# Some softmax reciprocals moved from VectorE to ScalarE, the instruction order given as a table, and the first loads reordered, in a two-layer linear-attention and gated-MLP kernel

## The chip, the core and the metric

The kernel runs on one core of a Trainium2 chip. The metric is the device time of one execution in microseconds (us). The engines are TensorE (PE, with its weight loads PEld), VectorE (DVE), ScalarE (ACT), GpSimd (POOL) and SyncE (SP), whose queue issues DMAs; ACT's queue issues some DMAs too.

## The reference

Inputs are bfloat16: `x` of 2048 rows by 512, and weights. Two blocks, A and B, alternate twice: A, B, A, B, each added to `x` after a layer normalisation without gain.

```python
# A: linear attention, H = 32 heads of Dh = 16
qkv = (x @ wqkv) ...                          # q, k, v: [b, h, s, d]
pq = einsum("bhsd,hdf->bhsf", q, w_phi);  pk = einsum("bhsd,hdf->bhsf", k, w_phi)
phi_q = concat([softmax(pq), softmax(-pq)]);  phi_k = concat([softmax(pk), softmax(-pk)])
kv = einsum("bhsf,bhsd->bhfd", phi_k, v);     z = einsum("bhsf->bhf", phi_k)
num = einsum("bhqf,bhfd->bhqd", phi_q, kv);   den = einsum("bhqf,bhf->bhq", phi_q, z)[..., None] + 1e-6
A = (num / den) @ wo
# B: gated MLP, F = 1376
gate = x @ W_gate;  up = x @ W_up
B = (gate * (gate > 0) * up) @ W_down
```

## The kernel before

`x` stays in SBUF as `X`, 16 tiles of 128 rows; four tiles are a chunk. For each layer:

- **Norm**: bn_stats and bn_aggr on DVE give mean and variance of a tile; POOL takes (variance + eps) to the power -1/2 into `rstd`; the tile is normalised on ACT, DVE or POOL and transposed, by a DMA of the SP queue or by PE. Some chunks of layer 1 take the two sums from accumulators instead (`sums`).
- **Folding**: the feature weights `w_phi` are multiplied into the key and query parts of `wqkv` (`Wk2`, `Wq2`), the key part by PE transposes, the query part by two DMA transposes of `wq`.
- **Keys and values** (`keys_values`, group k): PE projects a tile, ACT takes exp(p) and exp(-p) into `ek`, DVE (some of it after a halving add on POOL) sums each softmax into `sk`, DVE inverts the 128x64 sums into `rk`, and POOL and DVE share the scaling of `ek` by `rk`. PE adds up `kv` over all 16 tiles, values beside a column of ones (`vext`). `build_R` masks `kv` into `R` on DVE.
- **Queries** (`queries`, group q): the same with one scaling by the quotient of the two sums (`rq`), and a DMA transpose.
- **Attention** (groups a and p): PE multiplies by `R`; DVE inverts the denominators (`dd`) and scales; a transpose; PE multiplies by `wo`; DVE adds to `X`, with the row sum as accumulator; **Centre** takes the mean off.
- **The gated MLP** (`glu`, groups g and d): 10 column tiles of gate and up, by chunk, cut into parts (`PARTS`); ACT and DVE form the product; PE multiplies by `W_down`, DVE adds to `X`.

The program is first written down as a list of some 1,900 operations (`Plan.op`), each with engine, estimated time, what it reads and writes. `Plan.order` then walks through an estimated time and lets each engine take the ready operation with the highest rank, with a bias for each group and engine from the table `RANK`. The operations are emitted in that order; each engine runs its own in order. `STEP` holds, tile by tile, which engine does what: `kr` and `qr` the way of summing (`1` one DVE reduction over both halves, `2` two, `H` and `P` with one or two halving adds on POOL), `ks` how many of eight parts of the key scaling POOL takes, `part0` the cuts of the MLP chunks, `turn` which first tiles PE transposes, `wake` how many matmuls of zeros PE runs.

Of the kernel before, what the change touches and what calls it, by code (L numbers as in the profile page):

```python
# [8 lines left out]
P = 128  # L9
D = 512  # L10
H = 32
DH = 16
F = 1376
NDB = D // P
# [36 lines left out]
TAIL = {"PE": 0.165, "ACT": 0.12, "DVE": 0.115, "POOL": 0.045, "SP": 0.0}  # L51
SAME = {"PE": -0.165, "ACT": 0.035, "DVE": 0.035, "POOL": 0.08, "SP": 0.0}
HOPS = {("DVE", "POOL"): 0.09, ("ACT", "POOL"): 0.15}
NEXT = {"PE": 0.055, "SP": 0.03}
FREE = 0.06


def hop(a, b):
    return SAME[a] if a == b else HOPS.get((a, b), NEXT.get(b, 0.04))


class Plan:
# [10 lines left out]
    def op(self, eng, occ, fn, reads=(), writes=(), holds=(), lat=0.0, at=0.0, group=None, port=False, long=False):  # L73

        o = Op()
        o.eng, o.occ, o.cost, o.fn, o.lat, o.at, o.port, o.long = eng, occ, occ + TAIL[eng], fn, lat, at, port, long
        o.group, o.i_in = group or self.group
        base, slope = RANK.get(f"{o.group}.{eng}") or RANK[o.group]
        o.bias = base - slope * o.i_in
        o.preds, o.succs, o.i = set(), [], len(self.ops)  # L80
# [18 lines left out]
    def order(self):  # L99
        for o in self.ops:  # L100
            for p in o.preds:
                p.succs.append(o)
        for o in reversed(self.ops):
            o.rank = o.cost + o.lat + max([s.rank + hop(o.eng, s.eng) for s in o.succs], default=0.0)
        free = {k: [0.0] * n for k, (pool, n) in self.kinds.items()}
        engines = sorted({o.eng for o in self.ops})
        busy = {e: 0.0 for e in engines}
        ready = {e: [] for e in engines}
        for o in self.ops:
            o.wait, o.t0 = len(o.preds), o.at  # L110
            if not o.wait:
                ready[o.eng].append(o)
        seq, left, now, shut = [], len(self.ops), 0.0, 0.0
        while left:
            moved, later = False, []
            for e in engines:
                if busy[e] > now + 1e-9:
                    later.append(busy[e])
                    continue
                best = None  # L120
                for o in ready[e]:
                    if o.t0 > now + 1e-9:
                        later.append(o.t0)
                        continue
                    if o.port and shut > now + 1e-9:
                        later.append(shut)
                        continue
                    ok = True
                    need = {}
                    for b in o.bufs:  # L130
                        if b.slot is None:
                            need[b.kind] = need.get(b.kind, 0) + 1
                    for k, n in need.items():
                        got = [t for t in free[k] if t is not None]
                        if len(got) < n:
                            ok = False
                        else:
                            t = sorted(got)[n - 1]
                            if t > now + 1e-9:
                                later.append(t)  # L140
                                ok = False
                    if ok and (best is None or (o.rank + o.bias, -o.i) > (best.rank + best.bias, -best.i)):
                        best = o
                if best is None:
                    continue
                o = best
                ready[e].remove(o)
                moved, left = True, left - 1
                o.start, end = now, now + o.cost
                busy[e] = now + o.occ  # L150
                if o.long:
                    shut = end
                later.append(busy[e])
                for b in o.bufs:
                    if b.slot is None:
                        b.slot = min((i for i, t in enumerate(free[b.kind]) if t is not None),
                                     key=lambda i: free[b.kind][i])
                        free[b.kind][b.slot] = None
                        b.end = 0.0
                    b.left -= 1  # L160
                    b.end = max(b.end, end + o.lat + FREE)
                    if not b.left:
                        free[b.kind][b.slot] = b.end
                for s in o.succs:
                    s.wait -= 1
                    s.t0 = max(s.t0, end + o.lat + hop(e, s.eng))
                    if not s.wait:
                        ready[s.eng].append(s)
                seq.append(o)
            if not moved:  # L170
                later = [t for t in later if t > now + 1e-9]
                assert later, "the plan is stuck"
                now = min(later)
        self.seq = seq
        return seq
# [15 lines left out]
WF_IN, WK_IN, WV_IN, WQ_IN, LOADED = 3.4, 4.2, 6.7, 10.4, 11.0  # L191
X_IN = [3.3, 4.5] + [5.2] * 2 + [7.4] * 4 + [8.9] * 4 + [11.8] * 4
# [8 lines left out]
def setup(ctx, tc, A_x, A_wqkv, A_w_phi, A_wo, B_W_gate, B_W_up, B_W_down, out):  # L201
# [28 lines left out]
    nc.sync.dma_start(out=wkv[:, :, D:2 * D], in_=wv[:, :, 2 * D:3 * D])  # L230
    st.X, st.wkv, st.wq = X, wkv, wq

    st.zero = const.tile([P, D], BF16, name="zero")
    nc.vector.memset(st.zero[:], 0.0)
    wake = const.tile([P, 1], F32, name="wake")
    nc.scalar.activation(out=wake[:], in_=st.zero[:, 0:1], func=AF.Exp)
    nc.scalar.dma_start(out=X[:, 4:8, :], in_=xv[:, 4:8, :])
    nc.scalar.dma_start(out=X[:, 8:12, :], in_=xv[:, 8:12, :])
    nc.scalar.dma_start(out=wq[:], in_=wv[:, :, 0:D])
    nc.scalar.dma_start(out=X[:, 12:16, :], in_=xv[:, 12:16, :])  # L240
# [456 lines left out]
def keys_values(st, c, xnT, kv, L, last_er=()):  # L697

    nc, pl = st.nc, st.pl
    for ti in range(TPC):  # L700
# [21 lines left out]
        def invert(sk=sk, rk=rk):  # L722
            with nc.allow_low_precision(reason="the reference keeps a softmax and its sums in bfloat16"):
                nc.vector.reciprocal(out=rk[:], in_=sk[:])  # L724
# [284 lines left out]
```

## Time and profile before

| what | value |
|---|---|
| median of three runs | 381.89 us (381.57 to 382.64) |
| the profiled execution | 380.91 us, its span 379.2 us |
| busy: PE / DVE / ACT / POOL | 363.6 / 268.0 / 205.5 / 121.1 us |
| DMA, whole span | 32.61 MB, mean 86 GB/s |

The span is the time from the first to the last instruction in the trace; 1.7 us of the execution's own time lie outside it. Busy time is the union of an engine's instructions, an idle time is put down to what ended it.

### The profile page before, as it was taken

The numbers are of one execution on the slowest core, as the hardware profiler recorded it, in microseconds if no ns is written. First come the engines' busy times: TensorE is split into PE (matmuls) and PEld (weight loads), VectorE is DVE, ScalarE is ACT, GpSimd is POOL, SyncE is SP. The second block draws the span as 40 slices with busy tenths as digits, with TensorE's granted clock in tenths as the row PEclk, the third lists the DMA queues.
The fourth block names the chain that finished last, engine by engine and source line by source line (L and its number), as shares of the span: only waits on it lengthen the run. The fifth ranks groups of instructions, "written<-read, shape, count | busy, mean of one in ns | idle before, by whom it ended". The sixth has DMA issues, their size and how long they took to land.

```text
span 379.2 us, 6724 instructions
## 1 busy us (share of the span) xinstructions
PE 363.6 (96%) x2380; PEld 189.9 (50%) x2409; DVE 268.0 (71%) x608; ACT 205.5 (54%) x439; POOL 121.1 (32%) x203
## 2 busy tenths in 40 slices
PE   4898999999899999999999999999999999999996
PEld 2444545756445444444444456475654445454444
DVE  4999999999925442763497998999962675172433
ACT  4898979776762446737706925865234135514100
POOL 3798965131110220560155681724310002000000
PEclk9999999999999999999999999999999999999999
DMA  8889936788950230021013070478930075000011
GB/s 262 239 143 227 260 44 144 133 149 146 145 107 2 42 58 15 0 30 27 0 22 77 9 119 3 87 127 146 171 85 14 5 146 115 14 0 16 1 55 57
DMA packets 98882, 32.61 MB, mean 86 GB/s; under 512 B 90560, under 2 KB 98336, under 8 KB 98848
## 3 DMA queue, kind: packets, MB, share of 16 engines
q1 hardware_dynamic: 97216, 29.93, 39.7%
q10 hardware_dynamic: 1632, 2.24, 1.8%
q8 instruction: 19, 0.31, 0.4%
q14 instruction: 15, 0.12, 0.1%
HBM read 8.44 MB, written 2.10 MB: 28 GB/s over the span
## 4 chain that ended last, share of the span: by engine, by line
PE 64%; DVE 24%; DMA 6%; issue 2%; ACT 1%; POOL 1%; SPq 0%; POOLq 0%; ACTq 0%
PE ps L613 37%; PE ps L645 14%; PE ps L884 5%; DMA b<-b 4%; DVE sk L682 4%; DVE rk L724 3%; DVE bnst L388 3%; PE ps L794 3%; PE ps L593 3%; DVE sk L692 2%; DVE b L730 2%; PE q L833 2%; DMA X<-in_A_x_dram 2%; DVE sq L682 1%; DVE sk L688 1%
## 5 line engine op out<-in xcount | busy, mean ns | idle before, releaser
L613 PE MATMUL ps<-b,wu 128*128 128x512 bf16 (+2 forms) x400 | 79.2, 336 | 0.6 <-DMA b<-b 0.6
L613 PE MATMUL ps<-b,wg 128*128 128x512 bf16 (+2 forms) x400 | 78.6, 336 | 0.0
L645 PE MATMUL ps<-wd,b 128*128 128x512 bf16 (+3 forms) x368 | 78.1, 366 | 0.3
L623 ACT ACTIVATE b<-ps 128x512 bf16<-128x512 f32 (+2 forms) x100 | 50.5, 520 | 39.6 <-PE ps L613 39.1
L626 DVE SCALAR_TENSOR_TENSOR b<-ps,b 128x512 bf16<-128x512 f32 (+2 forms) x60 | 35.1, 598 | 39.9 <-PE ps L613 38.9
L645 PEld LDWEIGHTS <-b 128*128 128x128 bf16 (+1 forms) x374 | 35.3, 98 | 39.1
L613 PEld LDWEIGHTS <-wg 128*128 128x128 bf16 x400 | 36.1, 98 | 33.1
L613 PEld LDWEIGHTS <-wu 128*128 128x128 bf16 x400 | 36.2, 98 | 32.7 <-issue 0.9
L730 POOL TENSOR_TENSOR b<-b,rk 128x1024 bf16<-128x1024 bf16 (+6 forms) x28 | 37.5, 1351 | 9.6 <-DVE rk L724 7.9
L798 ACT ACTIVATE b<-ps 128x512 bf16<-128x512 f32 x64 | 33.0, 638 | 5.7 <-PE ps L794 5.1
L715 ACT ACTIVATE b<-ps 128x512 bf16<-128x512 f32 x64 | 33.7, 628 | 1.3 <-PE ps L710 1.3
L679 POOL TENSOR_TENSOR b<-b 128x256 f32<-128x256 bf16 x30 | 19.7, 670 | 43.9 <-ACT b L715 34.1
L570 DVE SCALAR_TENSOR_TENSOR X<-ps,r,X 128x512 bf16<-128x512 f32 (+2 forms) x26 | 18.2, 701 | 20.2 <-PE ps L645 20.1
L710 PE MATMUL ps<-Wk,b 128*128 128x512 bf16 x123 | 29.4, 379 | 2.0 <-DMA b<-b 1.2
L884 PE MATMUL ps<-wo,b 128*128 128x512 bf16 x118 | 29.7, 379 | 1.5 <-DMA b<-b 0.9
L630 DVE TENSOR_TENSOR b<-b,b 128x512 bf16<-128x512 bf16 (+2 forms) x40 | 13.5, 348 | 24.0 <-ACT b L623 22.3
L552 POOL TENSOR_SCALAR ve<-tot 128x4 f32<-128x4 f32 x8 | 1.9, 233 | 88.8 <-ACT sq L548 88.8
L663 PE MATMUL ps<-wkv,b 128*128 128x512 bf16 x122 | 29.9, 386 | 0.3
L794 PE MATMUL ps<-Wq,b 128*128 128x512 bf16 x126 | 29.5, 379 | 0.1
L548 ACT ACTIVATE sq<-b 128x512 bf16<-128x512 bf16 x32 | 20.1, 627 | 17.4 <-DVE b L527 17.0
L598 ACT CAST ur<-ps 128x192 bf16<-128x192 f32 (+1 forms) x18 | 5.4, 302 | 32.2 <-PE ps L593 32.1
L814 POOL TENSOR_TENSOR b<-b,rq 128x512 bf16<-128x512 bf16 x19 | 20.2, 1061 | 8.4 <-DVE rq L807 6.1
(94 smaller groups left out, 493.7 us busy)
## 6 DMA issues: line engine op xcount, KB each, us to landing
out_dram<-X SPq DMA_DIRECT2D x15, 128.0 KB, 1.8
X<-in_A_x_dram ACTq DMA_DIRECT2D x3, 512.0 KB, 7.2
b<-b SPq DMA_TRANSPOSE x94, 3.2
wg<-in_B_W_gate_dram SPq DMA_DIRECT2D x8, 160.0 KB, 3.2
wu<-in_B_W_up_dram SPq DMA_DIRECT2D x8, 160.0 KB, 4.0
wd<-in_B_W_down_dram SPq DMA_DIRECT2D x5, 256.0 KB, 4.7
wkv<-in_A_wqkv_dram SPq DMA_DIRECT2D x2, 512.0 KB, 7.1
wq<-in_A_wqkv_dram ACTq DMA_DIRECT2D x1, 512.0 KB, 8.3
```

The lines of the kernel that those rows point to most:

```text
L613: nc.tensor.matmul(ps[:], lhsT=wt[:, b, f * P:(f + 1) * P], rhs=xnT[:, lo:hi, b, :], start=(b == 0), stop=(b == NDB - 1))
L623: pl.op("ACT", 0.045 + 0.43 * share, lambda ups=ups, ru=ru, sign=1.0 if fuse else -1.0: nc.scalar.activation(out=ru[:], in_=ups[:], func=A ...
L626: pl.op("DVE", 0.06 + 0.548 * share, lambda gps=gps, ru=ru, h=h, cs=cs: nc.vector.scalar_tensor_tensor(out=h[:, cs], in0=gps[:], scalar=0. ...
L645: nc.tensor.matmul(yps[:], lhsT=hs[f][:fsz, ti * P:(ti + 1) * P], rhs=st.wd[:fsz, f, cols], start=(f == 0), stop=(f == NFT - 1))
L663: nc.tensor.matmul(vp[:], lhsT=xnT[:, ti, kb, :], rhs=st.wkv[:, kb, D:2 * D], start=(kb == 0), stop=(kb == NDB - 1))
L710: nc.tensor.matmul(ps[:], lhsT=xnT[:, ti, kb, :], rhs=w(kb), start=(kb == 0), stop=(kb == NDB - 1))
L715: pl.op("ACT", 0.48, lambda s=s, ek=ek, pk=pk: nc.scalar.activation(out=ek[:, :, s, :], in_=pk[:].rearrange("p (j x) -> p j x", j=8), func ...
L730: eng.tensor_tensor(out=phiK[:, lo:hi, :, :].rearrange("p j s (f h) -> p (j s) f h", h=4), in0=ek[:, lo:hi, :, :].rearrange("p j s (f h) - ...
L794: nc.tensor.matmul(pq[:], lhsT=xnT[:, ti, kb, :], rhs=st.Wq2[:, kb, :], start=(kb == 0), stop=(kb == NDB - 1))
L798: pl.op("ACT", 0.48, lambda s=s, eq=eq, pq=pq: nc.scalar.activation(out=eq[:, :, s, :], in_=pq[:].rearrange("p (j x) -> p j x", j=8), func ...
L814: (nc.vector if on_dve else nc.gpsimd).tensor_tensor(out=e, in0=e, in1=rq[:].unsqueeze(2).to_broadcast([P, 8, DH, 4]), op=Alu.mult)
L884: nc.tensor.matmul(yps[:], lhsT=turned(b), rhs=st.wo[:, b, :], start=(b == 0), stop=(b == NDB - 1))
```

## The change

It does six things.

1. Fourteen of the 32 inversions of key sums (nine in layer 0, five in layer 1) are taken as exp(-ln(s)) by two ACT instructions instead of a reciprocal on DVE (`ki0`, `ki1`), and three of the first normalisations take exp(-0.5 ln(v + eps)) there instead of a power on POOL (`rs`). One table set that has both functions is loaded by name at the start.
2. `Plan.order` no longer searches: the order of the 1,900 operations is the list `ORDER`, and buffers are given out along it. `RANK` and the estimates of waits go.
3. The estimated times are others: DVE's by measured spacing (for the reciprocal 0.46 for 0.415). With a fixed order they change nothing in the program.
4. The first loads go through other queues in another order, and the last two parts of `X` and `wq` are issued from within ACT's order (`LOAD_SP`, `LOAD_ACT`, `LATE`); the weight loads of the MLP and `wo` are placed one by one among SP's transposes.
5. The `STEP` strings are others: 26 matmuls of zeros for 3, more halving adds on POOL (39 for 30), fewer reductions over both halves (19 for 27), the first MLP chunk cut 1+1+2 instead of 1+3, three chunks of layer 1 with accumulated sums instead of two.
6. A path for raw keys is added that no tile takes (`raw` is 0).

```diff
-    nc.sync.dma_start(out=wkv[:, :, 0:D], in_=wv[:, :, D:2 * D])
-    nc.scalar.dma_start(out=X[:, 0:1, :], in_=xv[:, 0:1, :])
-    nc.scalar.dma_start(out=wf[:], in_=A_w_phi.rearrange("(b j) d f -> (j d) b f", b=NDB, j=8))
-    nc.sync.dma_start(out=X[:, 1:2, :], in_=xv[:, 1:2, :])
-    nc.sync.dma_start(out=X[:, 2:4, :], in_=xv[:, 2:4, :])
-    nc.sync.dma_start(out=wkv[:, :, D:2 * D], in_=wv[:, :, 2 * D:3 * D])
+LOAD_SP = ((0, 1), (1, 2))
+LOAD_ACT = ("f", "k", (2, 4), "v", (4, 8))
+LATE = ((8, 12), (12, 16), "q")
+    nc.scalar.add_instruction(mybir.InstLoadActFuncSet(name=nc.get_next_instruction_name(), act_func_set_id=LN_EXP, ins=[], outs=[]))
     nc.scalar.activation(out=wake[:], in_=st.zero[:, 0:1], func=AF.Exp)
...
+        by_log = STEP["ki" + L][t] == "A"
-        def invert(sk=sk, rk=rk):
+        def invert(sk=sk, rk=rk, by_log=by_log):
+            if by_log:
+                nc.scalar.activation(out=sk[:], in_=sk[:], func=AF.Ln)
+                nc.scalar.activation(out=rk[:], in_=sk[:], func=AF.Exp, scale=-1.0)
+                return
             with nc.allow_low_precision(reason="the reference keeps a softmax and its sums in bfloat16"):
                 nc.vector.reciprocal(out=rk[:], in_=sk[:])
-        pl.op("DVE", 0.415, invert,
+        pl.op("ACT" if by_log else "DVE", 0.36 if by_log else 0.46, dur=0.48 if by_log else 0.53, fn=invert,
               reads=[(sk, 0), (sk, 1)], writes=[(rk, 0)])
...
     def order(self):
...
+        self.seq = [self.ops[i] for i in ORDER]
+        for at, o in enumerate(self.seq):
...
+                if b.slot is None:
+                    free = [i for i, u in enumerate(owner[b.kind]) if u is None or not u.left]
+                    b.slot = min(free, key=lambda i: last[b.kind][i])
...
-    "part0": "4111", "part1": "6111", "tB0": "D---", "tB1": "--DA", "tA": "----", "wev": "ADADAAAAADDAAAAA",
-    "xn1": "ADAADDAPDAADDAAA", "turn": "A-AA", "wake": 3, "fuse0": "AFAA", "fuse1": "FFFF", "gate": 1, "sA": 2,
+    "raw": 0, "kev": "ADAD", "ki0": "ADDDDDDAAAADAAAA", "ki1": "DDDDADDDDDAAAADD", "qi0": "DDDDDDDDDDDDDDDD",
+    "qi1": "DDDDDDDDDDDDDDDD", "rs": "APPPPPPAPAPPPPPP", "part0": "3111", "part1": "6111", "tB0": "A---",
+    "tB1": "---A", "tA": "----", "wev": "DADDAAADDDDAAAAA", "xn1": "APADPAAPPAADAAAA", "turn": "ADAA", "wake": 26,
...
-RANK = {
-    "a0.DVE": (-27978.12, 47.27), "a0.PE": (4422.84, 62.03), "a1.DVE": (-3109.09, 76.61), "a1.PE": (-9282.73, -22.35),
...
+ORDER = [int(i) for i in """
+134 142 31 149 155 131 32 141 139 0 40 41 35 33 153 34 143 135 156 148 157 170 171 166 158 162 167 36 147 172 159 49
...
```

Three places show how the order moves. The first is the start of ACT's queue, up to the first evacuations of PSUM (`b`, `ps`): before,

```order
L226 DMA X<-in_A_x_dram 128x512
L227 DMA wf<-in_A_w_phi_dram 128x4x16
L236 ACT_TABLE_LOAD
L236 ACTIVATE wake<-zero 128x1
L237 DMA X<-in_A_x_dram 128x2048
L238 DMA X<-in_A_x_dram 128x2048
L239 DMA wq<-in_A_wqkv_dram 128x4x512
L240 DMA X<-in_A_x_dram 128x2048
L307 COPY b_130<-ps_131 128x512
```

and now:

```order
L164 DMA wf<-in_A_w_phi_dram 128x4x16
L164 DMA wkv<-in_A_wqkv_dram 128x4x512
L164 DMA X<-in_A_x_dram 128x1024
L164 DMA wkv<-in_A_wqkv_dram 128x4x512
L164 DMA X<-in_A_x_dram 128x2048
L174 ACT_TABLE_LOAD
L175 ACTIVATE wake<-zero 128x1
L164 DMA X<-in_A_x_dram 128x2048
L343 ACTIVATE ve_146<-mv_133,eps 128x1
L349 ACTIVATE rstd_150<-ve_146 128x1
L414 ACTIVATE b_204<-X,ve_186,rstd_150 128x512
L164 DMA X<-in_A_x_dram 128x2048
```

Both halves of `wkv` (keys, then values) now stand on ACT's queue ahead of most of `X`, and the logarithm and exponential of the first tile's variance stand between two loads.

The second place is SP's queue behind its first loads; `b` receives the transposed tiles. Before,

```order
L230 DMA wkv<-in_A_wqkv_dram 128x4x512
L490 DMA_TRANSPOSE b_207<-b_205 128x4x128
L337 DMA_TRANSPOSE b_274<-wq 128x8x128
L486 DMA_TRANSPOSE b_297<-b_277 128x8x128
L300 DMA wo<-in_A_wo_dram 128x512 x4
L300 DMA wr<-in_B_W_gate_dram 128x4x96
```

and now:

```order
L164 DMA X<-in_A_x_dram 128x512 x2
L280 DMA_TRANSPOSE b_398<-wq 128x8x128
L280 DMA_TRANSPOSE b_400<-wq 128x8x128
L440 DMA_TRANSPOSE b_443<-b_299 128x8x128
L444 DMA_TRANSPOSE b_469<-b_427 128x4x128
L440 DMA_TRANSPOSE b_469<-b_445 128x8x128
L243 DMA wg<-in_B_W_gate_dram 128x640
```

Both transposes of `wq`, which is now the last of the first loads, stand ahead of the first transposes of normalised tiles.

The third place is DVE at the first inversions of key sums (`sk` into `rk`). Before,

```order
L682 TENSOR_REDUCE sk_393<-b_249 128x64
L472 TENSOR_SCALAR b_412<-X,mv_321,rstd_377 128x512
L724 RECIPROCAL rk_416<-sk_393 128x64
L682 TENSOR_REDUCE sk_425<-b_267 128x64
L692 TENSOR_REDUCE sk_439<-b_325 128x8x4
L724 RECIPROCAL rk_450<-sk_425 128x64
L688 TENSOR_REDUCE sk_439<-b_395 128x8x4
```

and now:

```order
L700 RECIPROCAL rk_543<-sk_435 128x64
L706 TENSOR_TENSOR b_275<-b_274,rk_417 128x128
L700 RECIPROCAL rk_548<-sk_429 128x64
L333 BN_AGGR mv_535<-bnst_526 128x2
L706 TENSOR_TENSOR b_329<-b_328,rk_543 128x1024
L636 TENSOR_REDUCE sk_565<-b_486 128x64
L646 TENSOR_REDUCE sk_567<-b_495 128x8x4
L646 TENSOR_REDUCE sq_577<-b_505 128x8x4 x2
```

`rk_417` has no reciprocal here: ACT makes it, and sums of queries (`sq`) stand among those of keys.

More of the change, by code (lines that the diff above doesn't have):

```diff
@@ L47 @@
     pass
[L51 to L59, printed above, removed]
 class Plan:
@@ L99, in order @@
     def order(self):
[L100 to L173, printed above, removed]
@@ L296, in load_weights @@
     nc, seen = st.nc, {}
+    st.pl.rank("xl")
+    before = ()
+    for what, issue in st.late:
+        keys = [("wqin", 0)] if what == "q" else [("Xin", t) for t in range(*what)]
+        st.pl.op("ACT", 0.45, issue, reads=list(before), writes=keys, at=3.6, lat=2.0)
+        before = keys[:1]
     for n, (name, dst, src, kb) in enumerate(st.loads):
@@ L317, in wake @@
         z = Buf("ps", [P, D], F32)
[L318 removed]
+        pl.op("PE", 0.2155, lambda z=z: nc.tensor.matmul(z[:], lhsT=st.zero[:, 0:P], rhs=st.zero[:], start=True, stop=True),
               writes=[(z, 0)], at=1.2)
```

162 lines of the change are left out of this document (103 added, 59 removed), and 103 rows, old and new, of tables (ORDER, RANK, STEP).

## The prediction

> **What bounds the kernel now.** I read the page's busy times first, then the busy time by stage, then the chain that ended last, and for the start the instructions in order of time.
>
> ```profile
> PE 363.6 (96%) x2380; PEld 189.9 (50%) x2409; DVE 268.0 (71%) x608; ACT 205.5 (54%) x439; POOL 121.1 (32%) x203
> 0.00:10.00 10.00, 4.22 (x27) 2.68 (x27) 5.18 (x21) 4.33 (x7) 3.41 (x17) 1.00 0.82 267
> 10.00:20.00 10.00, 9.44 (x50) 4.79 (x52) 10.00 (x31) 8.87 (x17) 7.81 (x18) 1.00 0.86 229
> 20.00:55.00 35.00, 33.22 (x269) 17.24 (x272) 35.00 (x66) 30.96 (x61) 29.85 (x36) 1.00 0.74 172
> 64.00:96.00 32.00, 31.30 (x306) 20.78 (x308) 31.66 (x94) 23.24 (x66) 6.68 (x11) 1.00 0.81 146
> 100.00:110.00 10.00, 8.95 (x53) 4.58 (x53) 5.39 (x17) 9.25 (x24) 2.54 (x4) 1.00 0.78 124
> 110.00:150.00 40.00, 39.89 (x205) 19.38 (x205) 17.34 (x38) 17.41 (x37) 4.93 (x14) 1.00 0.18 34
> 240.00:260.00 20.00, 19.28 (x207) 12.65 (x207) 19.97 (x58) 12.76 (x35) 9.44 (x16) 1.00 0.68 115
> ```
>
> The columns behind the length of a stage are PE, PEld, DVE, ACT and POOL, then the granted clock, DMA share and GB/s. From 110 us on PE is full: whatever time is won or lost before that shifts the rest, and the end, by as much. Up to 96 us DVE is the full engine: 35.00 of 35 us, then 31.66 of 32. PE looks nearly full there too, but its busy time is a union of pipelined matmuls.
>
> ```profile
> 8.25 0.69 DVE bnst L388
> 19.61 1.10 DVE sk L682
> 22.57 0.59 DVE sk L692
> 23.16 0.46 DVE rk L724
> 31.72 0.53 DVE sk L688
> 166.86 17.27 PE ps L613 x80
> ```
>
> The chain (start, length) runs through DVE without a break worth naming from 8.25 to 51 us, and its pieces are the spacing of DVE's instructions: 1.10 for a reduction over both halves, 0.59 over one, 0.53 over a halved one, 0.46 for an inversion. The last line gives PE's spacing: 17.27 / 80 = 0.216 us for a matmul of 512 columns. All matmuls but the zeros, counted from the order by their columns at that price, make 357 us. So of the span's 379.2 us, 22 are not PE's work, and by the matmuls started in each 10 us, about 10 of these lie in the first 20 us, 8 between 20 and 110, 3 between 220 and 270, the rest at the end and in small gaps.
>
> **The start.** Here are the columns start, length.
>
> ```profile
> 1.24 1.46 PE L318 MATMUL ps<-zero 128*128 128x512 bf16 x3 [1.24 <-DVE zero L234]
> 1.73 1.28 ACT L236 ACT_TABLE_LOAD   x1 [1.73 <-PEq L993]
> 3.02 0.20 ACT L236 ACTIVATE wake<-zero 128x1 f32<-128x1 bf16 x1
> 3.86 0.69 DVE L388 BATCH_NORM_STATS2 bnst<-X 128x6 f32<-128x512 bf16 x1 [1.09 <-DMA X<-in_A_x_dram]
> 5.37 1.89 PE L351 MATMUL ps<-ident,wkv 128*128 128x128 bf16 x16 [2.66 <-DMA wkv<-in_A_wqkv_dram]
> 12.00 1.80 PE L663 MATMUL ps<-wkv,b 128*128 128x512 bf16 x4
> 17.29 3.63 PE L710 MATMUL ps<-Wk,b 128*128 128x512 bf16 x16 [0.46 <-ACT b L307]
> L230 SPq DMA_DIRECT2D wkv<-in_A_wqkv_dram x1: 442/442/442, 2.3 to 2.3; - x1
> DMA to landing us min/median/max: 9.6/9.6/9.6
> ```
>
> The value weights, issued at 2.3, land at 11.9, and the first value matmul starts at 12.00. Its four take 1.80 us (0.43 apart), where 16 later ones take 3.63 (0.22 apart). In the new order only the feature weights, the key half and 1 MB of `X` share the wires with the value half: some 2.0 MB, less the 0.5 MB of `X` queued behind it, is 1.5 MB at the 267 GB/s of the first row, 5.8 us from about 2 us on. An estimate: landing at 8 to 9. The first tile's normalised, PE-turned copy needs about as long, so the first value matmul should start near 9, 3 us earlier. Of this something goes back. Both transposes of `wq` now stand in SP's queue ahead of the first transposes of normalised tiles, and `wq` is the last of the loads.
>
> ```profile
> L398 POOL TENSOR_TENSOR rstd<-ve,mhalf 128x2 f32<-128x2 f32 x9 | 6.4, 714 | 0.1
> 12.19 1.23 SPq L337 DMA_TRANSPOSE b<-wq  x1
> 14.61 1.23 SPq L486 DMA_TRANSPOSE b<-b  x1
> ```
>
> Before, the first transposed pair was issued at 14.61. Now it waits for `wq` (the 3.3 MB of first loads end at 13 to 14.5 us at 230 to 267 GB/s) and two issues of 1.23: about 16.5. PE then has its first four tiles, which it turns itself, and waits again near 18 to 20. I take **-2.0 us** for the start, bounds 0 and -3.0.
>
> Twelve of the 26 zero matmuls stand in these gaps and three later; the first eleven at 0.43 end at about 6, when the key weights land (5.3 before, issued 0.45 earlier), so they cost nothing, or 0.7 at most. The three logarithm and exponential pairs for `rstd` replace POOL work off the chain; below nothing, they could save the 0.71 of a power, which lies inside the bounds above.
>
> The Trainium skill, "TensorE: Matmul & The Clock Gate" (Part 1), says that PE runs at half rate until busy for about 3.4 us, and falls back after an idle window of that length. The spacings agree, though the clock column says 1.00 in both stages. By that page the zeros keep PE at full rate and the whole -2.0 stands; if they did not, eight matmuls at 0.43 would cost 1.7 and the term would be -0.3, the forecast 380.8.
>
> **Keys to R, the middle stretch.** I counted each engine's work in the order between equal amounts of PE work, 12.3 and 42.5 us (the sixth key tile, and shortly before `R` is used), with these prices:
>
> ```profile
> L598 ACT CAST ur<-ps 128x96 bf16<-128x96 f32 x4 | 1.0, 249 | 0.3 <-PE ps L593 0.3
> PE ps L710 <- DMA b<-b: 1.2, 3, 0.5
> 14.70 2.07 ACT L715 ACTIVATE b<-ps 128x512 bf16<-128x512 f32 x4 [0.27 <-PE ps L710]
> L724 DVE RECIPROCAL rk<-sk 128x64 bf16<-128x64 f32 x32 | 16.6, 534 | 0.1
> L679 POOL TENSOR_TENSOR b<-b 128x256 f32<-128x256 bf16 x30 | 19.7, 670 | 43.9 <-ACT b L715 34.1 <-ACT b L798 9.6 <-DVE b L626 0.2
> L814 POOL TENSOR_TENSOR b<-b,rq 128x512 bf16<-128x512 bf16 x19 | 20.2, 1061 | 8.4 <-DVE rq L807 6.1 <-PE q L833 1.3
> L730 POOL TENSOR_TENSOR b<-b,rk 128x1024 bf16<-128x1024 bf16 x8 | 15.8, 1975 | 4.8 <-DVE rk L724 3.1 <-DVE mv L390 1.7
> ```
>
> Before: DVE 32.8 us, PE 30.0, ACT 27.0, POOL 25.1. After: POOL 32.5, ACT 31.8, DVE 31.5, PE 30.4. POOL gets seven more halving adds (0.67 each, 4.7) and two normalisations; ACT gets eight inversions and four more exponentials (2.07 / 4 = 0.5), and loses three copies. An inversion on ACT is not in this trace: its nearest rows are 0.20 us for one element and 0.25 for 96, so a pair costs 0.4 to 0.5; I take 0.45. What DVE gives up, 0.46 each, ACT takes on nearly whole. So one full engine becomes four nearly full ones that wait for each other in fixed order. Before, the stretch took about 32.5 us, DVE's own 32.8. Now the longest, 32.5, is the floor, and I add 2.5 us of waits: DVE lost nothing to three emptier engines (35.00 of 35), PE's projections waited 0.5 at most and three times, and five such waits on the chain, one for every second of ten key tiles, make 2.5. **+2.5 us**; bounds -0.3 (no waits) and +7.8 (a fifth of the time lost).
>
> **R to the end of the first MLP chunks.** From PE work 42.5 to 78.4: before, PE 36.2 and DVE 38.1; after, PE 36.4, DVE 32.7, ACT 24.7, POOL 17.4. DVE loses reductions over both halves (13 to 7 up to the first addition to `X`), reciprocals and normalisations, and gets more halved reductions. From the first `bn_stats` through the first addition to `X` its sum falls from 59.3 to 55.7 us, through the whole program from 258 to 248.
>
> ```profile
> 63.51 0.69 DVE L566 SCALAR_TENSOR_TENSOR X<-ps,X 128x512 bf16<-128x512 f32 x1
> 96.40 0.69 DVE L566 SCALAR_TENSOR_TENSOR X<-ps,X 128x512 bf16<-128x512 f32 x1 [0.15 <-PE ps L884]
> ```
>
> The sum is right for before: 3.86 (first `bn_stats`) plus 59.3 is 63.2, the addition ends at 64.2. PE becomes the bound behind this point, so what DVE cost over PE's own work goes: 38.1 less 36.4, 1.7, and from the 1.05 us that PE idles between 100 and 110 and the 0.70 between 64 and 96 most of the rest. **-3.2 us**; bounds 0 and -4.5. Cutting the first chunk 1+1+2 lets it start after two tiles at no further work but narrower matmuls (0.3 us).
>
> **Layer 1.** Between PE work 192 and 252 DVE falls from 59.3 to 51.7 us against PE's 60; PE idles 0.72 in the row from 240 to 260, a little before it. Five inversions and one more chunk of sums go to an ACT that is busy 12.76 of 20 us. **-0.8 us**, bounds 0 and -1.2. **PE's own work**: eight more transposes of 128 columns and narrower parts, **+0.7 us**; the three late zeros cost 0.6 at most.
>
> **The sum**: -2.0 + 2.5 - 3.2 - 0.8 + 0.7 = -2.8 us, from 380.91 of the profiled execution to 378.1. That execution is 1.0 below the median of the runs shown, so the forecast is **379.1 us**. A measurement can tell about 0.3% (1.15 us) from no change.
>
> **Rivals.**
>
> *Four full engines lock.* One chain of `ek`, sums, inversion, scaling goes through ACT, POOL, DVE and ACT again in fixed order, and a late step holds all that is queued behind it. If a fifth of the stretch is lost, it takes 40 us (+7.8), and the start of the MLP comes so late that only half of the third term is left: -2.0 + 7.8 - 1.6 - 0.8 + 0.7 = +4.1, 386.0. It turns slower where the stretch takes over 38 us. For it: POOL's 25.1 to 32.5, and DVE instructions that meet POOL's.
>
> ```profile
> L472 DVE TENSOR_SCALAR b<-X,rstd,ve x6: 408/414/1175, 133.7 to 165.2; 128x512 bf16<-128x512 bf16 x6
> ```
>
> One of six took 1175 ns where the median is 414. Against it: DVE's normalisations before the first addition to `X` fall from six to two. Chance 0.18. The Trainium skill, "SBUF — State Buffer" (SBUF: two separate sides), says that DVE and GpSimd share one pair of ports by an exclusive lock and the loser waits for the whole instruction, which speaks against more POOL work beside a full DVE; the 1175 ns agree with it.
>
> *SP's queue is late.* The last gate and up loads now stand behind the first query transposes, and the MLP's first matmul needs all of them.
>
> ```profile
> wu<-in_B_W_up_dram SPq DMA_DIRECT2D x8, 160.0 KB, 4.0
> ```
>
> A load lands 4.0 us after its issue; if its issue slips behind a transpose that waits for DVE, PE stands 4 us at the first chunk: +1.2 in all, 383.1. Chance 0.08.
>
> *Gains cancel.* The start brings 1 and the waits cost 4: 380.7 to 383.0, no change. Chance 0.13.
>
> *The waits vanish.* The stretch at its floor and the third term whole: -2.0 - 0.3 - 4.5 - 1.0 + 0.7 = -7.1, 374.8. Chance 0.10.
>
> That the table set is loaded again at each change of function (1.28 us) would add over 30 us to ACT, but the order holds one load: 0.01, counted as slower in the first rival's 0.18.
>
> **The numbers.** The forecast has 0.51; with the vanishing waits, faster is 0.61; no change 0.13; slower 0.26. The range from 375.0 to 385.5 leaves out half of the last case and two thirds of the lock, under 0.2.
>
> **What would show it.** Right: the first value matmul near 9 us, DVE's first addition to `X` ending near 62 (before 64.2), idle DVE time between 20 and 60, PE full from 65 on. Wrong: key inversions on ACT of over 0.6 us a pair, POOL rows of twice their length, the stretch over 38 us, or PE waiting for weights at the first MLP matmul.

## The result, and the profile after

The changed kernel takes 380.61 us (median, 379.81 to 381.11), the kernel before beside it 383.06 (381.25 to 384.36): a ratio of 0.9948 over the fast runs (the medians alone would give 0.9936), 95% interval 0.9926 to 0.9970. A second time it was 380.47 to 381.76, 0.9966 (0.9950 to 0.9982). It is faster by 0.3 to 0.5%; between the medians that is 1.3 to 2.5 us.

The two profiled executions say the opposite, 381.11 us after and 380.91 before, since the one shown of before is faster than all eleven times of that kernel (which spread over 3 us) and the one of after is its slowest. So both kernels were profiled again, and what follows uses both pairs.

Page and busy time by stage, after (columns as before: PE, PEld, DVE, ACT, POOL, clock, DMA share, GB/s):

```profile
span 379.4 us, 6902 instructions
PE 369.3 (97%) x2520; PEld 195.5 (52%) x2520; DVE 270.0 (71%) x598; ACT 211.6 (56%) x502; POOL 134.1 (35%) x220
0.00:10.00 10.00, 8.55 (x58) 4.32 (x59) 6.80 (x25) 5.33 (x10) 5.32 (x18) 1.00 0.83 256
10.00:20.00 10.00, 9.20 (x50) 4.21 (x47) 9.46 (x26) 9.14 (x22) 7.80 (x17) 1.00 0.73 177
20.00:55.00 35.00, 34.34 (x248) 17.13 (x248) 34.62 (x62) 34.07 (x77) 34.67 (x41) 1.00 0.79 168
64.00:96.00 32.00, 31.12 (x345) 23.13 (x344) 30.16 (x88) 24.56 (x84) 13.34 (x24) 1.00 0.56 101
100.00:110.00 10.00, 10.00 (x75) 5.91 (x74) 9.56 (x19) 6.72 (x17) 2.33 (x3) 1.00 0.77 111
240.00:260.00 20.00, 19.04 (x193) 12.07 (x192) 18.66 (x48) 16.37 (x44) 9.12 (x15) 1.00 0.58 95
```

From 20 to 55 us four engines are now full, POOL too (34.67 of 35, before 29.85). DVE hardly has more idle time than before, although its counted work there fell. From 100 to 110 us PE is now full (10.00, before 8.95), as hoped; from 64 to 96 and from 240 to 260 it still idles 0.9 and 1.0 us, no less than before (0.7 in both).

The instructions in order of time show the start, the one new wait of PE before `R`, `R` itself, and the first addition to `X`:

```profile
9.46 1.03 PE L617 MATMUL ps<-wkv,b 128*128 128x512 bf16 x4
14.49 3.40 SPq L280 DMA_TRANSPOSE b<-wq  x2
20.43 0.95 PE L307 MATMUL ps<-Wblk,b 128*128 128x128 bf16 x14 [0.95 <-DMA b<-wq]
56.30 0.91 PE L728 MATMUL q<-vext,b 128*128 128x68 bf16 x23 [1.16 <-DVE b L706]
58.01 0.79 DVE L750 TENSOR_TENSOR R<-M,q 128x272 bf16<-128x272 bf16 x2
63.45 0.69 DVE L520 SCALAR_TENSOR_TENSOR X<-ps,X 128x512 bf16<-128x512 f32 x1 [0.16 <-PE ps L868]
```

The first value matmul starts at 9.46 (before 12.00) and its four take 1.03 (before 1.80). But `R` starts at 58.01, where before it started at 52.90:

```profile
52.90 0.77 DVE L774 TENSOR_TENSOR R<-M,q 128x272 bf16<-128x272 bf16 x2
```

To see where time is won, I matched the matmuls of each trace to the order and added up their columns at 0.216 us for 512, without the zeros and with somewhat more than their share for the narrow ones (by columns alone the whole is 354.5 us before and 354.9 after). Each entry is the time at which PE had done so much of its own work; another price for the narrow ones moves the differences between the kernels by up to 0.7 us:

| PE's own work, us | before | before again | after | after again |
|---|---|---|---|---|
| 6 | 16.5 | 18.7 | 14.2 | 14.3 |
| 12 | 22.9 | 25.1 | 22.7 | 23.0 |
| 42 | 55.5 | 57.1 | 53.8 | 53.9 |
| 48 | 62.1 | 63.8 | 62.2 | 62.2 |
| 78 | 93.4 | 95.9 | 93.6 | 93.6 |
| 100 | 116.5 | 118.7 | 116.0 | 116.2 |
| 180 | 196.3 | 198.5 | 196.1 | 196.1 |
| 280 | 299.2 | 302.0 | 297.9 | 297.6 |
| 355 | 374.0 | 376.9 | 372.8 | 372.7 |
| span | 379.2 | 382.0 | 379.4 | 379.1 |

Won: 2.3 to 4.4 us by 6 us of work, of which 1.7 to 3.2 are left at 42. Lost: 1.6 to 1.8 between 42 and 48, the stretch around `R`, and 1.3 or 1.4 after 355. Won again: 1.1 to 2.0 in layer 1 (180 to 280: 102.9 and 103.5 before, 101.8 and 101.5 after).

### The profile page after: what moved, and what is told of

Read it like the earlier page. It is cut to its first block, busy times and chain, and to the rows that moved or that the text cites. A ratio compares the mean times of both kernels' runs of the same rounds, so it can differ in the third digit from the quotient of the medians.

```text
span 379.4 us, 6902 instructions
## 1 busy us (share of the span) xinstructions
PE 369.3 (97%) x2520; PEld 195.5 (52%) x2520; DVE 270.0 (71%) x598; ACT 211.6 (56%) x502; POOL 134.1 (35%) x220
## 4 chain that ended last, share of the span: by engine, by line
PE 78%; DVE 7%; POOL 5%; DMA 5%; ACT 3%; issue 1%; ACTq 0%; POOLq 0%
PE ps L567 34%; PE ps L599 19%; PE ps L868 6%; PE ps L770 5%; PE ps L617 4%; PE ps L664 4%; DMA b<-b 3%; PE ps L547 3%; POOL b L706 2%; PE q L817 2%; DMA X<-in_A_x_dram 2%; DVE b L706 1%; POOL b L633 1%; PE q L728 1%; ACT b L685 1%; DVE bnst L331 1%
## 5 line engine op out<-in xcount | busy, mean ns | idle before, releaser
L567 PE MATMUL ps<-b,wu 128*128 128x512 bf16 (+3 forms) x440 | 82.1, 321 | 0.0
L567 PE MATMUL ps<-b,wg 128*128 128x512 bf16 (+3 forms) x440 | 82.0, 321 | 0.0
L577 ACT ACTIVATE b<-ps 128x512 bf16<-128x512 f32 (+3 forms) x110 | 50.4, 484 | 55.7 <-PE ps L567 55.3
L567 PEld LDWEIGHTS <-wu 128*128 128x128 bf16 x440 | 38.7, 98 | 31.1
L706 POOL TENSOR_TENSOR b<-b,rk 128x1024 bf16<-128x1024 bf16 (+7 forms) x26 | 34.6, 1340 | 27.7 <-DVE rk L700 9.5
L774 ACT ACTIVATE b<-ps 128x512 bf16<-128x512 f32 x64 | 36.1, 619 | 11.8 <-PE ps L770 11.8
L685 ACT ACTIVATE b<-ps 128x512 bf16<-128x512 f32 x64 | 36.8, 631 | 5.9 <-PE ps L664 5.7
L633 POOL TENSOR_TENSOR b<-b 128x256 f32<-128x256 bf16 x39 | 26.5, 687 | 37.0 <-ACT b L774 17.5
L524 DVE SCALAR_TENSOR_TENSOR X<-ps,r,X 128x512 bf16<-128x512 f32 (+2 forms) x22 | 14.9, 698 | 25.0 <-PE ps L599 25.0
L617 PE MATMUL ps<-wkv,b 128*128 128x512 bf16 x128 | 31.7, 379 | 0.0
L520 DVE SCALAR_TENSOR_TENSOR X<-ps,X 128x512 bf16<-128x512 f32 x32 | 21.7, 681 | 11.3 <-PE ps L868 11.2
L798 POOL TENSOR_TENSOR b<-b,rq 128x512 bf16<-128x512 bf16 x22 | 24.2, 1108 | 3.5 <-DVE rq L791 2.6
L584 DVE TENSOR_TENSOR b<-b,b 128x128 bf16<-128x128 bf16 (+2 forms) x50 | 18.4, 399 | 7.4 <-ACT b L577 3.9
```

Of the source, the lines that this page charges most:

```text
L567: nc.tensor.matmul(ps[:], lhsT=wt[:, b, f * P:(f + 1) * P], rhs=xnT[:, lo:hi, b, :], start=(b == 0), stop=(b == NDB - 1))
L577: pl.op("ACT", 0.045 + 0.43 * share, lambda ups=ups, ru=ru, sign=1.0 if fuse else -1.0: nc.scalar.activation(out=ru[:], in_=ups[:], func=A ...
L617: nc.tensor.matmul(vp[:], lhsT=xnT[:, ti, kb, :], rhs=st.wkv[:, kb, D:2 * D], start=(kb == 0), stop=(kb == NDB - 1))
L633: nc.gpsimd.tensor_tensor(out=h[:].rearrange("p j f h -> p j (f h)"), in0=x[:, :, 0, :], in1=x[:, :, 1, :], op=Alu.add)
L685: pl.op("ACT", 0.48, lambda s=s, ek=ek, pk=pk: nc.scalar.activation(out=ek[:, :, s, :], in_=pk[:].rearrange("p (j x) -> p j x", j=8), func ...
L706: eng.tensor_tensor(out=phiK[:, lo:hi, :, :].rearrange("p j s (f h) -> p (j s) f h", h=4), in0=ek[:, lo:hi, :, :].rearrange("p j s (f h) - ...
```

## The experiments

Ratios are to the kernel before, on the same chip. The changed kernel itself was not timed beside most of these runs, and its own ratio came out as 0.9948 and 0.9966, so a difference of 0.7 us from it is not settled. Differences below are taken from 0.9966 or 380.47 us.

**Both kernels again.** No edit.

> The kernel before, profiled once more, since its eleven times spread over 3.1 us and its first profile was of the fastest. If the spread comes from the start (PE's clock and the landings), a slower execution loses its time before 20 us and is parallel to the first profile behind; if it comes from DVE's full stretch, DVE's rows between 20 and 96 us are longer; if from everywhere, PE's matmul spacing is over 0.216 us.

> The changed kernel once more, as the base of this study: 380.0 to 381.1 us, 0.992 to 0.997 of before, and a spread under 1.5 us.

The kernel before took 383.76 us in its one profiled run, span 382.0; the changed one 380.47, 0.9966. The busy time and the instructions of before's second run:

```profile
10.00:20.00 10.00, 8.71 (x40) 4.27 (x42) 10.00 (x32) 7.24 (x14) 7.82 (x17) 1.00 0.89 232
12.63 1.86 PE L663 MATMUL ps<-wkv,b 128*128 128x512 bf16 x4
14.29 2.34 PE L710 MATMUL ps<-Wk,b 128*128 128x512 bf16 x5
```

Values start 0.63 us later than in its first profile, and the next matmuls are still 0.43 apart. In the first profile the same matmuls are 0.22 apart:

```profile
13.63 1.89 PE L710 MATMUL ps<-Wk,b 128*128 128x512 bf16 x7
```

The spacing falls from 0.43 to 0.22 at 13.6 us in the first execution and only at 17.3 in the second. An estimate from this: 3.7 us at half the rate cost up to 1.8 us of PE's work, most of the lag. The clock column's 1.00 says nothing here, since the traces hold no clock record before 13.57 and 17.36 us. The second execution lags by 2.2 us at 6 us of work and by 2.8 at the end. So in these two most of before's spread arises in its start, while the two profiles of after, at the narrow spacing from 6.1 and 6.5 us on, agree there within 0.3.

**The tail.** The last addition in order of time: before, a quarter tile, and after, a whole one, written in one piece behind it:

```profile
376.36 0.35 DVE L570 SCALAR_TENSOR_TENSOR X<-ps,r,X 128x128 bf16<-128x128 f32 x1 [0.27 <-PE ps L645]
```

```profile
375.85 0.75 DVE L524 SCALAR_TENSOR_TENSOR X<-ps,r,X 128x512 bf16<-128x512 f32 x1 [1.63 <-PE ps L599]
```

```diff
 ORDER's end, the operations of the last tile's three pieces
-... 1880 1809 1875 1872 1876 1864 1865 1877 1866 1867 1868 1873 1874 1810 1811 1812 1869 1870 1871
+... 1809 1864 1865 1866 1867 1868 1810 1811 1812 1869 1870 1871 1872 1873 1874 1875 1876 1877 1878 1879 1880
```

> The changed kernel with the three pieces of the last tile moved to the end of the list, where the kernel before has them; nothing else moves. Theory (the end gives 0.7 us back because a whole tile is added and written last: 0.75 us and 128 KB for 0.35 us and 32 KB): 0.6 to 0.9 us less than the changed kernel. Rival (the last write is hidden or as long for a small piece): within 0.2 us.

379.78 us, 0.9945 (0.9924 to 0.9966): 0.7 us less than the changed kernel by the medians, near the quarter tile's gain, though the intervals overlap. From 355 us of work to the end it takes 5.6 us for 6.4.

**The zeros.**

```diff
-lambda z=z: nc.tensor.matmul(z[:], lhsT=st.zero[:, 0:P], rhs=st.zero[:], start=True, stop=True)
+(lambda z=z: nc.tensor.matmul(z[:], lhsT=st.zero[:, 0:P], rhs=st.zero[:], start=True, stop=True)) if i in (3, 11, 18) else (lambda: None)
```

> The changed kernel with only the first three of the 26 matmuls of zeros, all else in place. Theory (they keep PE at its full rate through the start): key transposes 1.9 us for 1.07, first value and key matmuls 0.43 apart, 1 to 2 us longer, and times that spread more. Rival (they only stand in gaps): within 0.3 us, or up to 0.6 us faster since three late ones are gone.

The three zeros that stay are not the first three of the queue: in the trace they run at 1.24, 1.64 and 17.55 us.

380.23, 0.9955 (0.9938 to 0.9971): no dearer. The first matmuls are slow again (16 transposes in 1.89 us for 1.07) and values start 1.1 us later,

```profile
6.43 1.89 PE L294 MATMUL ps<-ident,wkv 128*128 128x128 bf16 x16 [4.16 <-DMA wkv<-in_A_wqkv_dram]
10.54 1.03 PE L617 MATMUL ps<-wkv,b 128*128 128x512 bf16 x4
```

but by 18 us of work only 0.4 of that is left, since PE then waits for `wq`'s transposes anyway.

**All inversions on DVE**, the order kept.

```diff
-"ki0": "ADDDDDDAAAADAAAA", "ki1": "DDDDADDDDDAAAADD"
+"ki0": "DDDDDDDDDDDDDDDD", "ki1": "DDDDDDDDDDDDDDDD"
```

> The changed kernel with all 32 inversions of key sums on DVE again, each at the place in the list where ACT has it now. Theory (DVE still sets the time up to R, so what it gave up is what was gained): nine inversions of 0.46 come back before R, the first addition to X 3 to 4 us later, the whole 2 to 4 us longer. Rival (ACT and POOL are as full as DVE, and what DVE gives up ACT must do): the whole within 0.7 us of the changed kernel.

384.27, 1.0061 (1.0038 to 1.0084): against the changed kernel's 0.9966 that is 3.6 us slower. PE's waits, DVE's `R`, and two stretches by engine:

```profile
PE q L728 <- DVE b L706: 3.9, 2, 3.3
59.48 0.79 DVE L750 TENSOR_TENSOR R<-M,q 128x272 bf16<-128x272 bf16 x2 [0.36 <-PE q L728]
55.00:60.00 5.00, 2.04 (x34) 1.58 (x35) 4.61 (x12) 1.22 (x3) 2.27 (x5) 0.87 0.74 198
60.00:62.00 2.00, 2.00 (x13) 1.06 (x12) 0.78 (x2) 0.81 (x2) 2.00 (x5) 0.50 0.20 41
```

PE is level with the changed kernel up to 42 us of work (53.4) and needs 11.6 us for the next 6 instead of 8.4. PE's waits for the scalings grow from 1.5 to 3.9, and behind them the granted clock is 0.50 (60 to 62 us): the delay is paid twice, as a wait and as slower matmuls behind it.

**Inversions alone.** The kernel before with logarithms on ACT at the same tiles.

```diff
+LN_EXP = [s.name for s in act_sets.SETS].index("natural_log_exp_and_others")
+KI = {"0": "ADDDDDDAAAADAAAA", "1": "DDDDADDDDDAAAADD"}
...
+            if KI[L][t] == "A":
+                nc.scalar.activation(out=sk[:], in_=sk[:], func=AF.Ln)
+                nc.scalar.activation(out=rk[:], in_=sk[:], func=AF.Exp, scale=-1.0)
+                return
```

> The kernel before, in its own order, with the same 14 inversions taken as exp(-ln) on ACT at the same places, and the table set that has both. Theory (DVE was the only full engine, so 9 x 0.46 = 4.1 us less on it up to R is time): 2 to 3.5 us shorter than before. Rival (the order around it was made for DVE's inversions, ACT's in-order queue delays the pair behind exponentials, and the scaling waits for it): within 1 us, or longer.

383.94, 1.0052 (1.0030 to 1.0073): slower. Busy time, and a wait of PE that before did not have:

```profile
20.00:55.00 35.00, 32.24 (x268) 16.87 (x267) 31.91 (x54) 33.72 (x78) 28.13 (x34) 1.00 0.74 168
PE ps L802 <- ACT Wq L311: 1.6, 1, 1.6
```

DVE gets 3.1 us of idle time (31.91 for 35.00), and the time does not fall. The copy of `Wq` that ends PE's wait stands behind a pair in ACT's queue: the pair runs from 45.92 to 46.57, the copy at 46.47, where before the last of these copies ran at 43.86.

**The old load queues in the changed kernel.**

```diff
-LOAD_SP = ((0, 1), (1, 2))
-LOAD_ACT = ("f", "k", (2, 4), "v", (4, 8))
+LOAD_SP = ("k", (1, 2), (2, 4), "v")
+LOAD_ACT = ((0, 1), "f", (4, 8))
```

> The changed kernel with the first loads on the queues and in the order of before (key half, X, value half on SP; X, feature weights, X on ACT), the three late ones as now. Theory (the value half at 9.4 instead of 11.9 is the gain of the start): first value matmul near 12, the whole 1.5 to 2.5 us longer. Rival (PE waits for the query weights near 20 us in any case, so 2 us before that are lost there): 0 to 0.7 us longer.

383.09, 1.0033 (1.0012 to 1.0054): 2.6 us slower than 0.9966. `PE ps L617` now waits for the values until 12.12; behind this wait the trace's granted clock is 0.50 from 12.73 to 16.14 us, so this delay too is paid twice. 6 us of work are done at 18.1, and 3 us stay lost to the end (355 at 375.9).

```profile
PE ps L617 <- DMA wkv<-in_A_wqkv_dram: 1.5, 1, 1.5
```

**The new load queues alone**, in the kernel before.

```diff
-    nc.sync.dma_start(out=wkv[:, :, 0:D], in_=wv[:, :, D:2 * D])
-    nc.scalar.dma_start(out=X[:, 0:1, :], in_=xv[:, 0:1, :])
+    nc.sync.dma_start(out=X[:, 0:1, :], in_=xv[:, 0:1, :])
...
+    nc.scalar.dma_start(out=wkv[:, :, 0:D], in_=wv[:, :, D:2 * D])
+    nc.scalar.dma_start(out=X[:, 2:4, :], in_=xv[:, 2:4, :])
+    nc.scalar.dma_start(out=wkv[:, :, D:2 * D], in_=wv[:, :, 2 * D:3 * D])
+    nc.scalar.dma_start(out=X[:, 4:8, :], in_=xv[:, 4:8, :])
```

> The kernel before, order and reciprocals untouched, with the changed kernel's queues for the first loads: X's first two tiles on SyncE's queue; wf, key weights, X tiles 2 and 3, value weights, tiles 4 to 7, then the rest on ScalarE's queue. Theory 'the loads are the gain': putting the old queues into the changed kernel cost about 2.6 us, so the new queues alone bring 1.7 to 2.6 us, a ratio of 0.993 to 0.996, value products start near 9.5, and 6 us of TensorE work are done by 14 to 15 us instead of 16.5 to 18.7. Rival 'loads need the order': the order of the kernel before transposes query weights at 12 us and uses tile 0 for keys first; it waits for what now lands later, keeps under 1 us of the gain (0.998 to 1.001).

381.33, 0.9990 (0.9968 to 1.0011): nothing that can be told. The rival was right. Values start at 11.28 and still run 0.43 apart, behind folds and transposes at the same slow spacing:

```profile
6.05 1.89 PE L351 MATMUL ps<-ident,wkv 128*128 128x128 bf16 x16 [3.35 <-POOL rstd L398]
11.28 1.89 PE L663 MATMUL ps<-wkv,b 128*128 128x512 bf16 x4
```

**POOL less full.** Layer 0's halving additions emit nothing; DVE sums the full tiles at the same places.

```diff
-        pl.op("POOL", 0.62, add, ...
+        pl.op("POOL", 0.62, (lambda: None) if rank[-1] == "0" else add, ...
...
-in_=h[:].rearrange("p j f h -> p j h f")
+in_=e[:, :, s, :].rearrange("p j (f h) -> p j h f", h=4) if rank[-1] == "0" else h[:].rearrange("p j f h -> p j h f")
```

> The changed kernel without POOL's halving adds in layer 0; DVE sums the full halves instead, at the same places. Theory (DVE's key scalings, 1.07 us at 896 columns where they took 0.48 before, are held by POOL's work on the same SBUF): they fall to 0.5 to 0.6, some 2 us; DVE pays 0.08 for each of some 16 sums up to R, 1.3 us; the first addition to X comes 0.5 to 1.5 us earlier and the whole is 0.5 to 1.5 us shorter. Rival (the scalings are long for another reason, DVE's sum counts): 1 to 1.5 us longer.

381.64, 0.9990 (0.9971 to 1.0009): not faster than the changed kernel, rather 1 us slower, though the intervals overlap. POOL's busy time from 20 to 55 falls to 24.62, and yet a key scaling of DVE becomes longer. Its row holds one scaling of 384 columns (0.30) and one of 1024 that lasts 2.18 where 0.68 is usual; POOL's row is beside it:

```profile
20.00:55.00 35.00, 33.40 (x237) 16.88 (x238) 34.76 (x60) 32.98 (x76) 24.62 (x28) 1.00 0.76 176
31.67 2.39 DVE L706 TENSOR_TENSOR b<-b,rk 128x384 bf16<-128x384 bf16 x2
31.65 1.86 POOL L706 TENSOR_TENSOR b<-b,rk 128x896 bf16<-128x896 bf16 x1
```

POOL's ends at 33.51, DVE's at 34.06: it waited for the whole of it and then took its own 0.55. So what counts is not how full POOL is, but whether POOL is inside an instruction when the scaling starts. The changed kernel's trace has it both ways, here DVE behind POOL (POOL ends at 43.19, DVE at 43.67), then POOL behind DVE (1.72 for the usual 1.05):

```profile
41.73 1.94 DVE L706 TENSOR_TENSOR b<-b,rk 128x384 bf16<-128x384 bf16 x2
41.81 1.38 POOL L706 TENSOR_TENSOR b<-b,rk 128x640 bf16<-128x640 bf16 x1
47.59 0.62 DVE L706 TENSOR_TENSOR b<-b,rk 128x896 bf16<-128x896 bf16 x1
47.74 1.72 POOL L798 TENSOR_TENSOR b<-b,rq 128x512 bf16<-128x512 bf16 x1
```

This is the rule that the prediction took from the Trainium skill, "SBUF — State Buffer" (SBUF: two separate sides), for its first rival: an exclusive lock held for the whole instruction. The traces agree.

**Key scalings first.** Three query sums moved behind the last key scalings, which then fall into POOL's long ones.

```diff
 VectorE's operations around R in ORDER (364 and 365 are R)
-418 417 409 329 362 352 410 419 365 364
+329 362 352 418 417 409 410 419 365 364
```

> The changed kernel with one move in VectorE's order: three query sums (two of 512 columns, one of a halved tile, 1.77 us in the changed kernel's trace at 53.69 to 55.45) now stand behind the last three key scalings instead of ahead of them. Theory 'exclusive port': a key scaling that starts while GpSimd is inside an operation lasts until that operation has ended. GpSimd is busy without a gap from 51.92 to 55.48, so the first moved scaling takes 1.5 to 2.4 us instead of 0.60 or makes GpSimd's next one that much longer, the last scaling ends near 56.8 instead of 57.45, TensorE's two waits of 1.2 and 0.3 us for it shrink by 0.6 or 0.7, and the time falls by 0.2 to 0.6 us. Rival 'order only': the scalings take 0.60 each, end near 55.3, both waits go, and the time falls by 0.8 to 1.3 us. Rival 'given back': the query sums, now 1.8 us later, hold the first addition to X at 64.1, and the time stays within 0.2 us.

382.00, 1.0014 (0.9998 to 1.0029): slower than the changed kernel by 1.5 to 1.8 us, which none of the three had expected. In order of time:

```profile
53.89 1.52 DVE L706 TENSOR_TENSOR b<-b,rk 128x1024 bf16<-128x1024 bf16 x1 [0.67 <-ACT rk L697]
51.30 3.56 POOL L706 TENSOR_TENSOR b<-b,rk 128x896 bf16<-128x896 bf16 x2
58.89 0.72 DVE L750 TENSOR_TENSOR R<-M,q 128x272 bf16<-128x272 bf16 x2
60.01 1.89 PE L770 MATMUL ps<-Wq,b 128*128 128x512 bf16 x8
```

The lock is as foretold: POOL ends at 54.86, the scaling 0.55 later. The error was in the edit: the sums now stood between the scalings and `R`, which came at 58.89 in a run that had been 0.6 us ahead up to then, and PE needed 10.0 us from 42 to 48 of its work. It is one more run in which a later `R` goes with a later time behind it.

**Three edits together**: the tail, the zeros and the key scalings, each as above.

> The changed kernel with three edits at once: the last tile's split additions and writes at the very end of the order, only three late zero products kept, and the three query sums behind the last key scalings. If the parts add up: 0.7 us from the tail, 0.2 from the zeros, 0.2 to 0.6 from the scalings, thus 1.1 to 1.5 us below the changed kernel, a ratio to the kernel before of 0.992 to 0.994. If the scalings' edit is given back: 0.9 us, 0.994 to 0.995.

382.05, 1.0005 (0.9987 to 1.0023): they do not add up. The zeros that stay are the three of the run without zeros, none of them late. PE's wait for `R` is much the same as in the run just told (1.70 us), but the zero matmul that stood ahead of it is gone:

```profile
60.68 0.61 PE L817 MATMUL q<-R,b 128*128 128x68 bf16 x8 [1.70 <-DVE R L750]
61.10 3.28 PE L770 MATMUL ps<-Wq,b 128*128 128x512 bf16 x8
```

The eight matmuls behind it take 3.28 us; with the zero they took 1.89. The granted clock is 0.50 from 60.5 to 63.9 us here and 1.00 in the run just told. So one zero ahead of a late `R` goes with 1.4 us in these two traces, where leaving the zeros out cost nothing with `R` in time. No run changes that zero alone, so that it is the cause is not shown.

**POOL out of the way.** On the kernel with the tail, the halving addition at 56.02 moved 6 us back.

```diff
 GpSimd's operations behind the last key scaling in ORDER
-401 477 411 412 420 426 478 402 448
+401 411 412 420 426 478 402 477 448
```

> The changed kernel with its last split additions at the end of the order (0.7 us by an earlier run) and one move on GpSimd: the halving addition that ran at 56.02 to 56.77, in the middle of VectorE's last key scalings, now stands 6 us later, behind a query scaling; its sum is read at 66 us or later. Theory 'exclusive port': with GpSimd at rest the second of these scalings takes 0.68 us instead of 1.15, the last one ends 0.4 or 0.5 us sooner, TensorE's waits for them shrink from 1.5 to about 1.0 us, and the time is 0.3 to 0.5 us below the run with the tail alone, a ratio to the kernel before of 0.9925 to 0.994. Rival 'no port': the scaling stays near 1.15 us and the ratio at 0.9945. Rival 'given back': the scaling shortens, but the halving, now later, delays the query scalings behind it on GpSimd by 0.67 us and TensorE waits for those instead; the ratio stays at 0.9945 or above.

379.86, 0.9940 (0.9922 to 0.9959), the tail alone 0.9945. The three scalings, in the changed kernel

```profile
55.45 2.01 DVE L706 TENSOR_TENSOR b<-b,rk 128x1024 bf16<-128x1024 bf16 x3
```

now take 1.44, and POOL's small instruction (0.25 otherwise) is shut out for the whole of it:

```profile
55.46 1.44 DVE L706 TENSOR_TENSOR b<-b,rk 128x1024 bf16<-128x1024 bf16 x3
55.46 1.55 POOL L791 TENSOR_TENSOR rq<-sq 128x32 bf16<-128x32 f32 x1
```

No gain shows over the tail alone (the two ratios are well within each other's intervals), and the trace of that one says why: there DVE happened to get in first too,

```profile
55.19 1.42 DVE L706 TENSOR_TENSOR b<-b,rk 128x1024 bf16<-128x1024 bf16 x3
57.16 0.78 DVE L750 TENSOR_TENSOR R<-M,q 128x272 bf16<-128x272 bf16 x2
```

with `R` at 57.16. In all three traces the first scaling starts 0.03 or 0.04 us before POOL's long instruction ends; why POOL's small one then passes in the one and not in the other two is not shown. These two, 0.994, are the fastest versions found.

## Why the prediction was right, and which of its terms were not

The sign and the range held. The size held by the first measurement (-2.8 forecast, -2.45 between the medians) and not quite by the second (-1.3). That the sum came so near was luck: two terms missed by some 4 us each, in opposite directions, and both outside their own bounds. From the table, each difference for the first and the second pair of profiles:

| term | forecast | measured |
|---|---|---|
| start, to 12 us of PE's work | -2.0 | -0.2 / -2.1 |
| keys, 12 to 42 | +2.5 | -1.5 / -1.1 |
| `R` to the first MLP chunks, 42 to 100 | -3.2 | +1.2 / +0.7 |
| 100 to 180 | none | +0.3 / +0.1 |
| layer 1, 180 to 280 | -0.8 | -1.1 / -2.0 |
| 280 to 355 | none | +0.1 / +0.2 |
| end: PE's own work +0.7, and the tail | +0.7 | +1.4 / +1.3 |
| sum | -2.8 | +0.2 / -2.9 |

- **Start**: right in what it is (9.46 for "near 9", and PE waits for `wq`'s transposes at 20.43 as said). What it brings depends on which execution of before stands beside it, the one at half spacing until 13.6 us or the one until 17.3. Both halves are needed: the loads without the order bring nothing, the order without the loads is 2.6 us slower than with them. The prediction's sum without warm matmuls (380.8) fell: without the zeros the same place is 1.1 later, but the wait for `wq` takes it up.
- **Keys**: this step failed, outside its bounds of -0.3 and +7.8 (at the near one, if narrow matmuls are priced otherwise). "I add 2.5 us of waits" to a floor of 32.5 was wrong; 12 to 42 took 31.1 and 30.9, about DVE's own 31.5. The four engines are as full as was said (34.1 to 34.7 of 35 us each), but they did not hold each other up. Inversions on ACT cost 0.53 a pair, somewhat more than the 0.45 taken and under the 0.6 named as a sign of being wrong:

```profile
L696 ACT ACTIVATE sk<-sk 128x64 f32<-128x64 f32 x14 | 3.8, 274 | 2.2 <-DVE sk L636 1.1 <-DVE sk L646 0.9
L697 ACT ACTIVATE rk<-sk 128x64 bf16<-128x64 f32 x14 | 3.6, 257 | 0.8
```

- **`R` to the first MLP chunks**: this step failed, outside its bounds of 0 and -4.5. It let DVE's lighter load pass straight into time: "the first addition to X ending near 62". It ended at 64.14, as before, because DVE's load did not get lighter. Added up from the timelines without idle time, DVE's work from the first `bn_stats` through the first addition is 58.3 us before and 58.7 after, where the prediction counted 59.3 and 55.7. Inversions (-4.0) and normalisations (-1.4) did go. But DVE's key scalings grew from 5.1 to 8.8 us, since DVE took larger parts of them and since seven of them met an instruction of POOL. Copies, casts and sums took some 2 us more. By the lock the seven scalings took 2.7 us more than their usual length (before, two took 0.4 more), 1.1 of it the one at 41.99. Five of them fall ahead of 53.8 us, in the table's key stretch, and delay what follows through DVE's full queue.
- **`R` itself** comes 5.1 us later than before: 12 sums of queries (8.3 us) stand ahead of it on DVE, where before 4 did (3.1). The third piece shown ahead of the prediction has this order, and it was not followed to `R`. Among versions of the changed kernel the time goes with `R` (`R` at 57.16: 48 us of work at 61.7; 58.01: 62.2; 58.89: 63.2). It is not the whole of it, since the kernel before has `R` at 52.90 and 48 us of work at 62.1. No run moved those sums behind `R`.
- **The first rival** did not come: the stretch never neared its 38 us. The lock that it named as evidence is there, but its 2.7 us are about a third of the 7.8.
- **Layer 1**: the sign is right, the second pair outside the bounds of 0 and -1.2. The five inversions are not what gains there: with all inversions back on DVE, the stretch from 180 to 280 takes no longer than in the changed kernel. The rest of the term was not tested.
- **The signs** named as "right" came only in part: the first value matmul did, the first addition near 62 and idle DVE time between 20 and 60 did not, and PE is full only from 100 on, with gaps in layer 1. Two figures of the working are off without weight: by columns alone PE's work is 354.5 us, not 357, and the first loads are 3.7 MB, not 3.3.
- **The tail** was no term: the larger last piece costs about 0.7, as far as overlapping intervals can tell.

Open: what gains in layer 1 and why it is 1.1 in one pair and 2.0 in the other; what makes the first loads of the kernel before land 0.2 to 0.9 us later in its second profile, and the matmul spacing fall so much later there; and what the new ways of summing and the new cuts in `STEP` are worth, of which only the halving adds of layer 0 were tried.

## What to carry to other kernels

A new order, new load queues and work moved to another engine can each be worth nothing or less alone (1.005, 0.999) and pay together (0.995 to 0.997), so an engine's freed time must be followed through all else that this engine has to do, up to the step that PE waits for. Where DVE and GpSimd both read two SBUF operands, cost the overlap as one waiting for the whole instruction of the other, and place the steps on the path where GpSimd is not inside a long one. Profile both kernels twice before terms of 1 us are read from one pair.

## What the runs showed of the hardware

- Behind a wait of PE of 3.25 us the granted clock was 0.50 between 60 and 62 us; behind one of 1.51, with one of 1.05 ahead of it, it was 0.50 from 12.73 to 16.14; behind one of 1.70, with two short waits (0.95 and 0.36) ahead of it and no zero matmul between, eight matmuls took 3.28 us. Behind one of 1.48 with a zero matmul ahead of it they took 1.89.
- A 32-column instruction of GpSimd took 1.55 us instead of 0.25 while three DVE multiplications passed one after the other: the lock was not handed over between them.
- Two executions of the same program differed by 2.2 us in their first 20 us, and kept it. The spacing of matmuls of 512 columns fell from 0.43 to 0.22 us at 13.6 us in the one and at 17.3 in the other.
